# Three seams of an eight-expert block: order of row numbers, one late weight load, the counting product and the last weight halves

## The chip, the cores and the metric

The kernel runs on one core of a Trainium2 chip. The metric is device time in microseconds (us) of one execution; lower is better. Where a time is compared, it is the median over several executions of one kernel, or the time of the one execution that was profiled, and the text says which.

## What is computed

Three stages follow one another. The first is an attention over 4 batches x 8 heads x 576 positions x 64 (a coarse attention over means of 4 positions, plus a local one in a narrow band). Its result, read as 2304 tokens of 512, goes through a mixture of eight experts of which each token takes at most one, and then through a dense two-layer network with a gate. Cut to what matters here:

```python
def _moe_ref(x, w_skip, w_gate, w1, w2):              # 2304 tokens, 512 wide, 8 experts, 1024 hidden
    do_compute = x @ w_skip > 0
    xc = x[do_compute]
    logits = xc @ w_gate
    e_idx = argmax(logits);  gate_w = softmax(logits)[e_idx]
    for e in range(8):
        mask = e_idx == e
        h = maximum(xc[mask] @ w1[e], 0.0)
        y[mask] = gate_w[mask, None] * (h @ w2[e])
    out[do_compute] = xc + y

def _moe2_ref(x, w_in, w_out):                        # 512 -> 2048 -> 512
    h = x @ w_in
    return (h / (1 + exp(-1.702 * h))) @ w_out
```

## The kernel before

**Stages.** Phase A (0 to about 165 us) computes the attention in 16 units (four per batch), writes each unit's tokens to a table `xd` in device memory (`xn` tiles, `L644`), and after the last unit of a batch decides for each token its expert and its place in that expert's list. Phase B (about 165 to 345 us) does the experts. An overflow loop behind it handles tokens beyond an expert's 192 places; its count of passes comes out zero here. Phase C (to the end, 727 us) is the dense network.

**Numbers.** Weights are f32 in memory and are used as two f16 parts: `wh`, the high part (scaled by a power of two, `w_s`), and `wl`, what is left. For each expert there are four half matrices of 1 MB: first layer halves 00 and 01, second layer halves 10 and 11. Each is loaded by SP (`raw`, `L935`), run through a sum of squares on ACT (`jk`, `L951`, function `bound`), from which a small product on PE (`psw`, function `scale`) and six short DVE instructions (`w_e`, `w_s`, `w_i`, and `iv`; function `scale2`, step `scb`) make the scale; then `wh` (`hi`, `L975` on ACT, `L977` on DVE) and `wl` (`lo`, `L983`, always DVE). `scale(i)` makes the scale of expert i's second layer together with that of expert i+1's first layer. The tokens have one scale for all, `sx_s`, made from their largest value `xb` (`xb0` to `xb4`, ending with `xmax`, `L789`).

**An expert's steps.** POOL gathers an expert's 192 token rows (`g0` with 128 rows by the row numbers `idt`, `g1` with 64 rows by `idu`, `L1017`). PE transposes them (`px`, `L1030`, `L1033`), ACT makes the high part `xh` (`L1039`), DVE the low part `xl` (`L1045`). The first layer is three products (`wh xh`, `wh xl`, `wl xh`) into `ph` (`L1063`); ACT makes `hh`, DVE `hl`; the second layer (`py`, `L1086` for the 128 rows and `L1101` for the 64) is scaled by `giv` (gate times scales, `L1110`) into `yr` on ACT, added to the gathered row on POOL (`yadd`) and scattered back to `xd`. For the last expert DVE does `yadd` itself from `py` (`L1142`).

**Row numbers.** `ids` (four DVE instructions, `L766` to `L769`) turns the sums `sa` over all batches into `idt` and `idu`. In phase B, DVE's first `wl` is held behind the instruction that `ex.first` names; before, that is the last of `ids` (`L769`). Its first `wh` (step `hi00` of expert 0) is not held.

**What sets the order.** In phase A a planner walks all steps with priorities and estimated durations and writes the order of every engine; a load is a step that may name others that it waits for (the list with `("xd", ...)` at `L1692`). In phase B each step has a due time in the table `STAGE_B` (in experts, e plus the entry), with exceptions in `head` (expert 0), `mine` (expert 1) and `tail` (expert 7); the steps sorted by these times are the order for PE, ACT, DVE and POOL. SP's own order is chosen when the program is built, by an estimate of when what a transfer waits for is done. At most four groups of table writes of phase A are in flight at a time. `passes` (one product `pc` on PE, four DVE instructions `L1148` to `L1156`) counts the overflow passes from the tokens per expert, `acc`, which are final at the end of phase A; `count` loads the result into a register. It stands at time -1.0, which on DVE is behind `giv` of expert 0 and ahead of `xl` of expert 2.

**Beside the experts,** the weights of phase C are prepared within phases A and B (`win.load`, `win.high`, `win.join`, `win.square`: the `w` and `jw` instructions of `L231` to `L256`).

Of the kernel before, what the change touches and what calls it, by code (L numbers as in the profile page):

```python
# [18 lines left out]
P = 128  # L19
# [358 lines left out]
def phase_a(ctx, tc, c, qk, v, vwin, ex, win, fill, tidy):  # L378
# [382 lines left out]
    def ids(b):  # L761

        z = cp.tile([P, 2, E], F32, name="idz")
        d, d2 = cp.tile([P, 2, E], I32, name="idt"), cp.tile([P, E], I32, name="idu")
        a = c["sa"]
        V.tensor_scalar(z, a[:, :, 1, :], 0.0, float(NT + TB), op0=ALU.is_equal, op1=ALU.mult)  # L766
        V.scalar_tensor_tensor(z, a[:, :, 1, :], float(TB), z, op0=ALU.mult, op1=ALU.add)
        V.scalar_tensor_tensor(d, z, -float(TB), a[:, :, 0, :], op0=ALU.add, op1=ALU.add)
        c["idi"] = V.tensor_scalar(d2, d[:, 1, :], 2.0, c["hf2"], op0=ALU.mult, op1=ALU.add).ins  # L769
        c["id"] = d[:, 0, :], d2  # L770
# [16 lines left out]
    def xb4(u):  # L787
        c["sx"], c["ix"] = pow2_scale(nc, cp, hd["ps"][:, P:P + 1], "sx", True, t=XT)
        V.tensor_scalar(c["xmax"], c["ix"], 2.0 ** XT, None, op0=ALU.mult)  # L789
# [110 lines left out]
    for i, rd in ((-1, (0, 1)), (0, (2, 3, 4, 5))):  # L900
        add(es, i, [("eb", j) for j in rd] + ([("xb4", NU - 1)] if i == 0 else []), [("es", "small", 2)])
        add(ev, i, ["es"], [("ev",)])
# [16 lines left out]
class Experts:  # L919
# [50 lines left out]

    def hi(self, e, wi, hf, on_act):
# [4 lines left out]
        else:  # L976
            self.nc.vector.tensor_scalar(t, r, s, None, op0=ALU.mult)  # L977
        self.h[e, wi, hf] = t

    def lo(self, e, wi, hf):  # L980
# [3 lines left out]
        if self.first is not None:  # L984
            self.tc.add_manual_dep(i.ins, self.first.name,
                                   mybir.DependencyInfo(mybir.DependencyClass.NoSync, mybir.DependencyReason.DATA),
                                   reason="row numbers first")
            self.first = None
# [3 lines left out]
def phase_b(ctx, tc, c, ex, win, wout):  # L992
# [15 lines left out]
    ex.first = c["idi"]  # L1008
# [195 lines left out]
    done += [(0, "scale"), (0, "scb")]  # L1204
    tail = dict(l2b0=-1.23735, l2b1=-1.23734, giv=-1.64, yadd0=-1.22, scatter0=-1.21, ymx=-0.59)
# [9 lines left out]
    for i, t in zip(range(WA, DF // P), (4.5, 4.51, 4.52, 4.53, 5.1, 5.11, 5.12, 5.13)):  # L1215
# [6 lines left out]
    sched.append((-1.0, -2, 0, lambda e: passes()))  # L1222
# [394 lines left out]
def kern(ctx: ExitStack, tc, qk, v, vwin, w_gate, w1, w2, w_in, w_out, out):  # L1617
# [66 lines left out]
    with ab:  # L1684
# [4 lines left out]
        with ea as s:  # L1689
            fill = [(6.4, init, "SP", 0.45, 0.1, (), 0), (-7.6, init1, "SP", 1.3, 0.4, [("xd", 0)], 1)]  # L1690
            fill += [(5.5 + 4 * e + 2 * wi + hf, lambda e=e, wi=wi, hf=hf: [ex.load(e, wi, hf)], "SP", 0.4, 2.75,
                      [("xd", LOADS_A["e"][4 * e + 2 * wi + hf])] + [("wd", j) for j in range(WA // 2) if e == 0], (e, wi, hf))  # L1692
# [62 lines left out]
```

## Time and profile before

| | |
|---|---|
| median of 3 runs | 728.62 us (725.91 to 729.83) |
| the profiled execution | 728.87 us |
| its span, first to last instruction | 727.2 us |
| mean granted PE clock over the span | 0.960 of 2.4 GHz |
| PE busy | 654.9 us, 90% of the span |
| DVE busy | 494.4 us, 68% |
| ACT busy | 425.6 us, 59% |
| POOL busy | 221.5 us, 30% |

A share of busy time is a mean over three stages with different limits. Phase C, more than half of the span, is nearly all PE. The change lies in the stretch from about 118 to 340 us, so the views to read are those of that stretch: the timeline of each engine, which gives an instruction's start, its length, and in brackets the idle time ahead of it and what ended that; the busy time in short windows with the granted clock; and the chain, which starts at the last instruction and follows back what each step waited for.

### The profile page before, as it was taken

What the parts mean: (1) busy time and instruction counts of PE and PEld (TensorE: products, weight loads), DVE (VectorE), ACT (ScalarE), POOL (GpSimd) and SP (SyncE); (2) the same over time, 40 slices, a digit from 0 to 9 for tenths busy, and PEclk for the clock granted to TensorE, in tenths of its full rate; (3) what the DMA queues carried; (4) which work ended last, traced back from release to release, by engine and by line L of the source; (5) the groups of instructions that cost most, each with busy time, mean ns of one, the idle gap of its engine ahead of it and who ended that gap; (6) DMA issues with size and microseconds to landing.
All of it is one profiled execution on the core that took longest, in us unless ns stands there. A gap on an engine that the chain in (4) does not pass through costs nothing.

```text
span 727.2 us, 16364 instructions
## 1 busy us (share of the span) xinstructions
PE 654.9 (90%) x6639; PEld 460.9 (63%) x6639; DVE 494.4 (68%) x1027; ACT 425.6 (59%) x891; POOL 221.5 (30%) x216
## 2 busy tenths in 40 slices
PE   4788988773889999975999999999999999999997
PEld 3576878663767777753666665444974795695443
DVE  6589898865669999977898999975544365063000
ACT  4478787783785888683779794242544364163111
POOL 6686754205546787781000002411000000000000
PEclk9899999975999999997999999999999999999999
DMA  8799976853747777644240411000011000100111
GB/s 302 235 300 294 280 207 224 274 168 109 234 171 274 247 284 283 216 157 129 76 145 16 174 59 43 16 30 29 16 26 47 16 2 15 29 2 1 30 30 30
DMA packets 37889, 94.90 MB, mean 131 GB/s; under 512 B 8861, under 2 KB 22817, under 8 KB 31668
## 3 DMA queue, kind: packets, MB, share of 16 engines
q1 hardware_dynamic: 34996, 88.34, 37.0%
q0 software_dynamic: 2816, 5.50, 2.5%
q8 instruction: 53, 0.87, 0.5%
q14 instruction: 24, 0.20, 0.1%
HBM read 81.91 MB, written 12.92 MB: 130 GB/s over the span
## 4 chain that ended last, share of the span: by engine, by line
PE 55%; DVE 18%; issue 11%; ACT 6%; DMA 6%; POOL 4%; SPq 0%; POOLq 0%; ACTq 0%; DVEq 0%
PE po L1534 17%; PE ph L1437 13%; PE px L1474 7%; DVE wl L983 3%; PE py L1474 3%; PE ph L1063 3%; DMA xd<-xn 3%; DVE v L1406 2%; PE po L576 2%; POOL ids L1172 2%; PE pz L1474 2%; PE px L628 1%; POOL g L1139 1%; DVE wh L977 1%; PE px L1355 1%
## 5 line engine op out<-in xcount | busy, mean ns | idle before, releaser
L1534 PEld LDWEIGHTS <-gh 128*128 128x128 f16 x576 | 56.2, 98 | 66.4 <-issue 1.3
L983 DVE SCALAR_TENSOR_TENSOR wl<-raw,w_s,wh 128x2048 f16<-128x2048 f32 x32 | 76.5, 2422 | 7.8 <-ACT wh L975 6.9
L1437 PE MATMUL ph<-xx,wih 128*128 128x384 f16 x384 | 72.6, 326 | 0.8 <-ACT xx L1369 0.8
L1542 ACT ACTIVATE o<-po,os 128x128 f32<-128x128 f32 x72 | 20.6, 369 | 83.3 <-issue 55.4
L1534 PE MATMUL po<-woh,gh 128*128 128x512 f16 x288 | 65.9, 379 | 1.0 <-ACT o L1542 1.0
L1534 PE MATMUL po<-wol,gh 128*128 128x512 f16 x288 | 65.6, 379 | 0.0
L1534 PE MATMUL po<-woh,gl 128*128 128x512 f16 x288 | 65.4, 379 | 0.0
L951 ACT ACTIVATE jk<-raw 128x2048 f16<-128x2048 f32 x32 | 61.1, 1911 | 6.4 <-issue 4.9
L1403 POOL TENSOR_TENSOR v<-wih,wil 128x512 f32<-128x512 f16 x16 | 18.4, 1151 | 141.4 <-ACT gh L1429 108.0
L1437 PEld LDWEIGHTS <-wih 128*128 128x128 f16 x384 | 37.7, 100 | 23.9 <-issue 1.0
L1534 PEld LDWEIGHTS <-gl 128*128 128x128 f16 x288 | 28.2, 98 | 33.5
L1063 PEld LDWEIGHTS <-wh 128*128 128x128 f16 x512 | 44.6, 101 | 6.4 <-issue 5.4
L975 ACT ACTIVATE wh<-raw,w_s 128x2048 f16<-128x2048 f32 x18 | 35.2, 1995 | 20.0 <-DVE w_s L80 17.3
L1485 DVE TENSOR_TENSOR q<-pz,q 128x192 f32<-128x192 f32 x24 | 8.6, 358 | 54.7 <-ACT q L1483 49.1
L1437 PE MATMUL ph<-xx,wil 128*128 128x384 f16 x192 | 39.2, 326 | 0.0
L1139 POOL TENSOR_TENSOR g<-g,yr 128x512 f32<-128x512 f32 (+1 forms) x14 | 30.3, 2162 | 26.8 <-ACT yr L1123 26.6
L1441 ACT ACTIVATE sg<-ph,ih 128x384 f32<-128x384 f32 x48 | 27.7, 577 | 17.0 <-PE ph L1437 16.2
L1063 PE MATMUL ph<-xh,wl 128*128 128x192 f16 x256 | 33.2, 253 | 2.8 <-DVE wl L983 1.8
L1430 DVE SCALAR_TENSOR_TENSOR gl<-sg,gs,gh 128x384 f16<-128x384 f32 x48 | 31.0, 646 | 6.3 <-ACT gh L1429 6.0
L1063 PE MATMUL ph<-xl,wh 128*128 128x192 f16 x256 | 33.5, 254 | 1.9 <-DVE xl L1045 1.1
L1474 PEld LDWEIGHTS <-sh 128*128 128x128 f16 x384 | 34.0, 98 | 1.2 <-issue 0.5
L1063 PE MATMUL ph<-xh,wh 128*128 128x192 f16 x256 | 33.5, 255 | 1.2 <-ACT xh L1039 1.0
(262 smaller groups left out, 1649.3 us busy)
## 6 DMA issues: line engine op xcount, KB each, us to landing
raw<-in_moe_w SPq DMA_DIRECT2D x32, 1024.0 KB
vw<-in_vwin SPq DMA_DIRECT2D x16, 576.0 KB
qk<-in_qk SPq DMA_DIRECT2D x16, 576.0 KB
w<-in_moe_w_in SPq DMA_DIRECT2D x8, 1024.0 KB
w<-in_moe_w_out SPq DMA_DIRECT2D x8, 1024.0 KB
vn<-in_v SPq DMA_DIRECT2D x16, 288.0 KB
xd<-xn SPq DMA_DIRECT2D x16, 288.0 KB
x<-xd SPq DMA_DIRECT2D x18, 256.0 KB
```

The lines of the kernel that those rows point to most:

```text
L951: self.nc.scalar.activation(j, r, AF.Square, accum_out=self.mx[i][:, hf, wi:wi + 1])
L975: self.nc.scalar.activation(t, r, AF.Copy, scale=s)
L983: i = self.nc.vector.scalar_tensor_tensor(t, r, s, self.h[e, wi, hf], op0=ALU.mult, op1=ALU.subtract)
L1063: T.matmul(ph[:, fi, :], wa[:, k_, o:o + P], xa[:, k_, :], start=(n == 0), stop=(n == 3 * NK - 1))
L1139: G.tensor_tensor(g, g, yr[e][:, cols(ti)].rearrange("p (h w) -> p h w", w=DM // 2), ALU.add)
L1403: G.tensor_tensor(v, h, l, ALU.add)
L1430: V.scalar_tensor_tensor(split[2], split[0], split[3], split[1], op0=ALU.mult, op1=ALU.subtract)
L1437: T.matmul(ph, win.chunk(wa, f)[:, k_, :], xx[:, k_, :], start=(n == 0), stop=(n == 3 * NK - 1))
L1441: A.activation(sg, ph, AF.Gelu_apprx_sigmoid, scale=ih[:, f // 4:f // 4 + 1])
L1474: T.matmul(o, w[:, k_], xx[:, at + k_], start=(first and i + k_ == 0), stop=(i + k_ == 3), skip_group_check=not first)
L1534: T.matmul(po, ga[:, f, i * P:(i + 1) * P], wa[:, f, :], start=(n == 0), stop=(n == 3 * (DF // P) - 1))
L1542: A.activation(o[:, sl], po[:, sl], AF.Copy, scale=os_[:, j:j + 1])
```

## The change

It has five parts.

1. Phase B's first `wh` and first `wl` on DVE are both held behind `xmax`, the last instruction of the token scale, instead of the first `wl` alone behind `idu`.
2. The scale of expert 0's second layer and expert 1's first layer leaves the plan of phase A and becomes a step of phase B like those of the other experts.
3. The load of expert 1's second first-layer half (1, 0, 1) waits for the last batch's gates (`("gs", B - 1)`, the `gt` tiles).
4. `passes` moves from -1.0 to -5.97, among the first steps of phase B.
5. For expert 7, `scb`, `hi11` and `lo11` come earlier, so that both second-layer halves are made in one go, and the eight `win.high` steps come later.

```diff
 def ids(b):
-        c["idi"] = V.tensor_scalar(d2, d[:, 1, :], 2.0, c["hf2"], op0=ALU.mult, op1=ALU.add).ins
+        V.tensor_scalar(d2, d[:, 1, :], 2.0, c["hf2"], op0=ALU.mult, op1=ALU.add)
 def xb4(u):
-        V.tensor_scalar(c["xmax"], c["ix"], 2.0 ** XT, None, op0=ALU.mult)
+        c["last"] = V.tensor_scalar(c["xmax"], c["ix"], 2.0 ** XT, None, op0=ALU.mult).ins
...
-    for i, rd in ((-1, (0, 1)), (0, (2, 3, 4, 5))):
-        add(es, i, [("eb", j) for j in rd] + ([("xb4", NU - 1)] if i == 0 else []), [("es", "small", 2)])
-        add(ev, i, ["es"], [("ev",)])
+    add(es, -1, [("eb", 0), ("eb", 1)], [("es", "small", 2)])
+    add(ev, -1, ["es"], [("ev",)])
...
+    def in_turn(self, i):
+        if self.first is not None:
+            self.tc.add_manual_dep(i.ins, self.first.name,
+                                   mybir.DependencyInfo(mybir.DependencyClass.NoSync, mybir.DependencyReason.DATA),
+                                   reason="row numbers and scale first")
+            self.first = None
 def hi(self, e, wi, hf, on_act):
-            self.nc.vector.tensor_scalar(t, r, s, None, op0=ALU.mult)
+            self.in_turn(self.nc.vector.tensor_scalar(t, r, s, None, op0=ALU.mult))
...
-    ex.first = c["idi"]
+    ex.first = c["last"]
...
-    done += [(0, "scale"), (0, "scb")]
-    tail = dict(l2b0=-1.23735, l2b1=-1.23734, giv=-1.64, yadd0=-1.22, scatter0=-1.21, ymx=-0.59)
+    tail = dict(scb=-2.2805, hi11=-2.11, lo11=-1.891, l2b0=-1.23735, l2b1=-1.23734, giv=-1.64, yadd0=-1.22, scatter0=-1.21, ymx=-0.59)
...
-    for i, t in zip(range(WA, DF // P), (4.5, 4.51, 4.52, 4.53, 5.1, 5.11, 5.12, 5.13)):
+    for i, t in zip(range(WA, DF // P), (5.272, 5.273, 5.274, 5.275, 5.276, 5.277, 5.39, 5.41)):
         word(t, win.high, i)
...
-    sched.append((-1.0, -2, 0, lambda e: passes()))
+    sched.append((-5.97, -2, 0, lambda e: passes()))
...
-                      [("xd", ...)] + [("wd", j) for j in range(WA // 2) if e == 0], (e, wi, hf))
+                      [("xd", ...)] + [("wd", j) for j in range(WA // 2) if e == 0] + [("gs", B - 1)] * (hf == e == 1), (e, wi, hf))
```

What moves on the engines is shown at three places.

**SP, end of phase A.** `xd<-gt_97` are the last batch's gates, `raw` the experts' weights, `TENSOR_LOAD tot` the register load of the overflow count. Lines with - stand in the kernel before, lines with + in the changed one.

```order
 L755 DMA xd<-gt_97 96x6x8 x2
-L935 DMA raw<-in_moe_w 128x2048 x6
-L1160 TENSOR_LOAD tot
-L1160 ISA x2
-L935 DMA raw<-in_moe_w 128x2048 x16
+L934 DMA raw<-in_moe_w 128x2048 x3
+L1162 TENSOR_LOAD tot
+L1162 ISA x2
+L934 DMA raw<-in_moe_w 128x2048 x22
```

Twenty-two loads stood behind the gates and 25 stand there now. The three that are new there stood, before, some ten transfers further up, between the load of `w_2271` and a write `xd<-xn`, as `L935 DMA raw<-in_moe_w 128x2048 x3`: (1, 0, 1) and the two first-layer halves of expert 2, which wait for nothing. The register load has three weight loads ahead of it behind the gates, where it had six.

**DVE, where phase A ends and phase B begins.** First the kernel before, from the token maximum `xb`; then, before still, the place of the counting instructions, behind `giv` of expert 0; then the changed kernel, from `t_2947` on.

```order
L774 TENSOR_REDUCE xb<-xm 128x1
L977 TENSOR_SCALAR wh<-raw,w_s 128x2048
L723 TENSOR_TENSOR sa<-sa,sel 128x32
L766 TENSOR_SCALAR idz<-sa 128x16
L767 SCALAR_TENSOR_TENSOR idz<-sa,idz 128x16
L768 SCALAR_TENSOR_TENSOR idt<-idz,sa 128x16
L769 TENSOR_SCALAR idu<-idt,hf_102 128x8
L782 TENSOR_REDUCE xb_2930<-psm 1x1
L729 SCALAR_TENSOR_TENSOR t_2932<-mn,r_2212 96x6
L983 SCALAR_TENSOR_TENSOR wl<-raw,w_s,wh 128x2048
```

```order
L1110 TENSOR_TENSOR giv<-g_3004,iv 128x1
L1110 TENSOR_TENSOR giv<-g_3005,iv 128x1
L1148 COPY cnt<-pc 128x8
L1151 TENSOR_TENSOR gt<-cnt,thr 128x136
L1154 TENSOR_REDUCE sums<-gt 128x1
L1156 CAST tot<-sums 128x1
L1045 SCALAR_TENSOR_TENSOR xl<-px,sx_s,xh 128x768
L983 SCALAR_TENSOR_TENSOR wl<-raw,w_s,wh 128x2048 x2
```

```order
L729 SCALAR_TENSOR_TENSOR t_2947<-mn,r_2877 96x6
L983 TENSOR_SCALAR wh<-raw,w_s 128x2048
L730 TENSOR_TENSOR t_2947<-t_2947,cf 96x6
L989 SCALAR_TENSOR_TENSOR wl<-raw,w_s,wh 128x2048
L1150 COPY cnt<-pc 128x8
L731 TENSOR_SCALAR slt<-t_2947 96x6
L729 SCALAR_TENSOR_TENSOR t_2951<-mn,r_2667 96x6
L1153 TENSOR_TENSOR gt<-cnt,thr 128x136
L730 TENSOR_TENSOR t_2951<-t_2951,cf 96x6
L1156 TENSOR_REDUCE sums<-gt 128x1
L731 TENSOR_SCALAR slt<-t_2951 96x6
L1158 CAST tot<-sums 128x1
```

The row numbers (`sa` to `idu`) and the token scale (to `xmax`) now stand ahead of the first `wh`, and the four counting instructions stand behind the first `wl`, ahead of expert 0's `xl`, instead of ahead of expert 2's. On PE the product `pc` moves likewise, from behind the first layer of expert 1 to just ahead of expert 0's `px`.

**ACT, the last expert.** `w_4629` to `w_4880` are weights of phase C, `wh` here the second-layer halves of expert 7, `yr` the results of expert 6. First before, then changed.

```order
L1069 ACTIVATE hh<-ph 128x384 x2
L252 ACTIVATE w_4629<-w_4629 128x512 x2
L252 ACTIVATE w_4631<-w_4631 128x512 x2
L975 ACTIVATE wh<-raw,w_s 128x2048
L1123 ACTIVATE yr<-py,giv 128x512
L1123 ACTIVATE yr<-py,giv 128x256
L1069 ACTIVATE hh<-ph 128x384
L252 ACTIVATE w_4878<-w_4878 128x512 x2
L252 ACTIVATE w_4880<-w_4880 128x512
L1069 ACTIVATE hh<-ph 128x384
L252 ACTIVATE w_4880<-w_4880 128x512
L975 ACTIVATE wh<-raw,w_s 128x2048
```

```order
L1071 ACTIVATE hh<-ph 128x384 x2
L981 ACTIVATE wh<-raw,w_s 128x2048 x2
L1125 ACTIVATE yr<-py,giv 128x512
L1125 ACTIVATE yr<-py,giv 128x256
L1071 ACTIVATE hh<-ph 128x384 x2
L252 ACTIVATE w_4629<-w_4629 128x512 x2
L252 ACTIVATE w_4631<-w_4631 128x512 x2
L252 ACTIVATE w_4878<-w_4878 128x512 x2
L252 ACTIVATE w_4880<-w_4880 128x512 x2
```

Both `wh` stand together ahead of `yr`, and the eight instructions for phase C behind the last `hh`. On DVE the scale steps of the last expert come ahead of two `hl`, and the two `wl` follow one another.

## Rows read from the trace of the kernel before

**Rows 1.** Page, section 4: share of each engine in the chain that ended last

```profile
PE 55%; DVE 18%; issue 11%; ACT 6%; DMA 6%; POOL 4%; SPq 0%; POOLq 0%; ACTq 0%; DVEq 0%
```

**Rows 2.** The chain, 110 to 185 us: start, us, engine, what

```profile
121.93 12.41 DMA xd<-xn
...
161.26 4.72 DMA xd<-gt
```

**Rows 3.** Timeline, SP: start, us of issuing, transfer, count

```profile
118.93 2.38 SPq L935 DMA_DIRECT2D raw<-in_moe_w  x3
...
156.50 0.45 SPq L935 DMA_DIRECT2D raw<-in_moe_w  x1
...
160.91 0.88 SPq L755 DMA_DIRECT2D xd<-gt  x2
```

**Rows 4.** Windows: stretch, us, busy PE, PEld, DVE, ACT, POOL, clock, DMA, GB/s

```profile
120.00:123.00 3.00, 3.00 (x96) 2.71 (x94) 2.86 (x10) 2.99 (x7) 0.00 (x0) 1.00 1.03 420
147.00:150.00 3.00, 2.44 (x11) 2.47 (x12) 2.23 (x15) 2.78 (x8) 0.00 (x0) 0.50 0.03 5
188.00:192.00 4.00, 2.07 (x12) 1.11 (x10) 3.71 (x2) 2.21 (x3) 3.14 (x3) 0.89 0.22 35
229.95:247.63 17.68, 17.68 (x187) 13.93 (x185) 16.83 (x21) 14.93 (x18) 13.37 (x8) 1.00 0.81 298
```

**Rows 5.** Timeline of ACT, DVE and POOL, 140 to 190 us

```profile
140.69 0.80 ACT L638 COPY xn<-px 96x768 f32<-96x768 f32 x1 [1.06 <-DMA xd<-xn]
164.11 1.91 ACT L951 ACTIVATE jk<-raw 128x2048 f16<-128x2048 f32 x1 [1.13 <-DMA raw<-in_moe_w]
166.09 2.00 ACT L975 ACTIVATE wh<-raw,w_s 128x2048 f16<-128x2048 f32 x1
176.62 0.90 ACT L1039 ACTIVATE xh<-px,sx_s 128x768 f16<-128x768 f32 x1 [6.63 <-PE px L1033]
...
166.46 1.29 DVE L977 TENSOR_SCALAR wh<-raw,w_s 128x2048 f16<-128x2048 f32 x1 [3.28 <-DMA xd<-gt]
168.30 0.17 DVE L768 SCALAR_TENSOR_TENSOR idt<-idz,sa 128x16 int32<-128x16 f32 x1
168.92 2.33 DVE L983 SCALAR_TENSOR_TENSOR wl<-raw,w_s,wh 128x2048 f16<-128x2048 f32 x1
...
169.55 2.75 POOL L1017 DMA_INDIRECT g<-xd,idt  x1 [10.59 <-DVE t L729]
172.60 0.95 POOL L1017 DMA_INDIRECT g<-xd,idu  x1 [0.30 <-DVE sx_i L81]
189.50 1.94 POOL L1172 DMA_INDIRECT ids<-tok,slt  x1 [0.31 <-issue]
```

**Rows 6.** Timeline of ACT, DVE and PE around the counting product, 204 to 219 us

```profile
204.43 3.90 ACT L975 ACTIVATE wh<-raw,w_s 128x2048 f16<-128x2048 f32 x2 [2.21 <-DVE w_s L80]
...
210.27 0.17 DVE L1148 COPY cnt<-pc 128x8 f32<-128x8 f32 x1 [5.41 <-PE pc L1147]
...
212.26 0.49 PE L1063 MATMUL ph<-xl,wh 128*128 128x192 f16 x4 [0.86 <-DVE xl L1045]
214.53 0.51 PE L1063 MATMUL ph<-xh,wl 128*128 128x192 f16 x4 [1.77 <-DVE wl L983]
...
215.98 0.85 PE L1063 MATMUL ph<-xh,wl 128*128 128x192 f16 x4
```

**Rows 7.** Timeline of ACT, DVE and PE in the last expert, 314 to 335 us

```profile
321.78 2.00 ACT L975 ACTIVATE wh<-raw,w_s 128x2048 f16<-128x2048 f32 x1
...
314.77 0.15 DVE L75 TENSOR_SCALAR w_e<-psw 128x2 int32<-128x2 int32 x1
323.82 3.08 DVE L983 SCALAR_TENSOR_TENSOR wl<-raw,w_s,wh 128x2048 f16<-128x2048 f32 x1 [1.68 <-ACT wh L975]
334.90 0.48 DVE L1142 SCALAR_TENSOR_TENSOR g<-py,giv,g 128x256 f32<-128x256 f32 x1 [0.52 <-DVE w L233]
...
326.95 0.59 PE L1086 MATMUL py<-wl,hh 128*128 128x512 f16 x2 [2.52 <-DVE wl L983]
```

More of the change, by code (lines that the diff above doesn't have):

```diff
@@ L983, in lo @@
         i = self.nc.vector.scalar_tensor_tensor(t, r, s, self.h[e, wi, hf], op0=ALU.mult, op1=ALU.subtract)
[L984 to L988, printed above, removed]
+        self.in_turn(i)
         self.l[e, wi, hf] = t
@@ L1691, in kern @@
             fill += [(5.5 + 4 * e + 2 * wi + hf, lambda e=e, wi=wi, hf=hf: [ex.load(e, wi, hf)], "SP", 0.4, 2.75,
-                      [("xd", LOADS_A["e"][4 * e + 2 * wi + hf])] + [("wd", j) for j in range(WA // 2) if e == 0], (e, wi, hf))
+                      [("xd", LOADS_A["e"][4 * e + 2 * wi + hf])] + [("wd", j) for j in range(WA // 2) if e == 0] + [("gs", B - 1)] * (hf == e == 1), (e, wi, hf))
                      for e in range(2) for wi in range(2 - e) for hf in range(2)]
```

## The prediction

> **What bounds the kernel now.** I read three views in this order. The chain's shares by engine [rows 1]: PE holds 55% of the way to the last instruction, DVE 18%, transfers 6%, and "issue" 11%. PE's part is mostly the dense network, which the change does not touch, so the question is what PE waits for earlier. The busy windows answer it: in the middle of the experts PE is busy 17.68 of 17.68 us per expert, at clock 1.00 (2.4 GHz), while DVE has 16.83 [rows 4]. There PE cannot be helped; a gain must come from places where PE waits or has a low clock. The timelines show four: the seam from attention to routing, where a table write sits 12.41 us behind loads [rows 2] and PE runs at clock 0.50 (1.2 GHz) afterwards [rows 4]; the first gather, for which everything in the experts waits [rows 5]; the counting product, which leaves DVE idle for 5.41 us [rows 6]; and the last expert, where PE waits 2.52 us for a `wl` [rows 7]. The sum goes against the profiled execution, 728.87 us; the median is 728.62, so the two can be taken as one.
>
> **Part by part.**
>
> *The late load.* Before, a load of phase C's weights and three expert loads, 4 MB, stand ahead of the write issued at 121.93 [rows 2, 3]; at the 420 GB/s of the next window [rows 4] 4 MB take 10.0 us, which is most of its 12.41. ACT then waits 1.06 us for that write before its next `xn` [rows 5]. The order shows that 3 of the 4 MB go, some 7.5 us, so this write ends well before ACT asks. Taken: -1.1 us, the wait itself. Bounds: 0, if the next wait swallows it; and -3.6, if PE also keeps a higher clock there. The window at 147 has clock 0.50 with 2.44 of 3 us busy [rows 4]; at the full clock about half of that, with waits kept, returns in two such stretches, 2.5 us. I take the end nearer the wait, because PE falls to 0.50 after waiting for a chain of DVE and ACT steps that stays.
>
> The same 3 MB now start behind the gates, whose write is issued at 160.91 and takes 0.88 [rows 3], thus at about 161.8, beside the first gathers. At 420 GB/s they take 7.5 us; the load of 156.50 ended when ACT's `jk` could start at 164.11 [rows 3, 5], so the three end at about 167 to 172 (estimate). ACT has a `jk` that reads the first of them (1.91 us) and a `wh` (2.00) [rows 5] ahead of `xh`: 167.6 + 0.2 + 4 gives 171.8, while `xh` can start at 176.62 less the gain of the next step, 174.3. Cost 0, with 2.5 us of cover.
>
> *Row numbers first.* Before, DVE's first `wh` started at 166.46, when the gates had landed (161.26 + 4.72 = 165.98), and `idt` came behind it at 168.30 to 168.47 [rows 2, 5]. The gather needs both the gates and `idt`. After, `idt` stands ahead of `wh` and is ready before the gates, so the release moves from 168.5 to about 166. The gather itself began at 169.55 and took 2.75 us while DVE ran `wl` (168.92 to 171.25); the second, with DVE at other work, took 0.95, and a third POOL transfer at 189.50, beside a `wl`, took 1.94 [rows 5]. So a gather started beside a long DVE instruction ends with it. After, the first starts at 166.5, together with `wh` (to 167.75), and ends about 168.7; the second meets `wl`, which now ends at 170.3, and ends at 171.2, against 173.55. Gain 2.35. Bounds: -4.85, if neither is held (171.2 less 2.5), and +0.1, if the short DVE instructions that now stand first (twenty of about 0.17 us) delay `wh`. Behind the gathers everything to the first product moves: `px`, `xh`, `ph`. I take -2.35, since the two rows with a `wl` beside the transfer agree.
>
> By the Trainium skill's page "SBUF — State Buffer", section "SBUF: two separate sides", a VectorE instruction with two SBUF inputs and a GpSimd one lock each other out of a shared port for the whole instruction, and a software-issued transfer cannot write its descriptors meanwhile. The rows of 2.75 against 0.95 agree. By the strict form the gathers would wait for both `wh` and `wl`; this is the third rival below.
>
> *The scale of expert 0's second layer.* Two products and seven DVE instructions (about 1.4 us) move behind expert 0's first `hl`. They are the same work; `wh` of the second layer needs them only after the first layer. Cost 0, bounded by +0.9 if PE must wait once more as it did for `xl` [rows 6].
>
> *The counting product.* DVE's copy stands idle 5.41 us for `pc`, which PE reaches only behind expert 1's first layer; `xl` of expert 2 and two `wl` stand behind it. PE then waits 0.86 and 1.77 us and, after that, falls to a lower clock: groups of four matmuls take 0.85 us against 0.49 [rows 6]. Four such groups cost 4 x 0.36 = 1.4, their slower neighbours some 0.3. Moved to the head, the copy waits for nothing: `acc` is final long before, and its four instructions (some 0.9 us) lie between `wl` and `xl` at 171 to 172, while DVE waits for `xh` anyway. At expert 2, DVE gains more (ACT's second `wh` ends at 208.33, so the second `wl` could move from 214.6 to 208.8, 5.8 us), but PE, which is full before 210 and after 219, returns only its own loss: 0.86 + 1.77 + 1.7 and the wait within the groups, 4.3 to 4.6. Taken: -4.5. Bounds: -2.6 (the two waits, clock as before) and -6.35 (5.41 and the four instructions, if DVE were the bound).
>
> On SP the register load of the count now has only three loads ahead of it and waits for DVE until about 172; the next load behind it waited before for the gathers until past 173. Cost 0.
>
> *The last expert.* Before, ACT's second `wh` ran at 321.78 to 323.78, `wl` started at 323.82, took 3.08, and PE waited 2.52 for it; the end of the chain is DVE's last `yadd`, at 334.90 [rows 7]. After, the scale steps start some 0.9 us before 314.77 (two `hl` no longer stand ahead), ACT makes both `wh` at about 315 to 319, DVE both `wl` at 317 to 321.6, then `hl`, `ym`, `hl` to 323.5. The three joins and two `yadd` that follow stood from 326.9 to 335.4; they now start at 323.8, three us earlier, and PE is ready for them since its wait is gone. `yr` of expert 6 comes 1.0 us later; POOL's add and scatter behind it end well before DVE's last `yadd`. Gain 3.3. Bounds: -2.3, if POOL's add slows DVE's pair of `wl` to 3.08 each; -5.0, if the 0.5 us waits between the joins go too.
>
> **Sum:** -1.1 - 2.35 - 4.5 - 3.3 = -11.25; 728.87 - 11.25 = 717.6 us. The dense network behind it keeps its length, give or take 1.5 us, since there PE's order changes in small places only.
>
> **The rivals.**
>
> - *More comes back at the head* (0.15). Between 188 and 192 PE is busy only 2.07 of 4 us, with waits that no other instruction ends [rows 4]. If this goes away with the new timing, or the clock holds at the seam, 3.6 us more: 714.0. Against it: nothing in the change removes instructions there.
> - *The seams are eaten* (0.13). The three loads and the gathers run together, and `jk` on the late load stands first on ACT; if that gives back exactly the first two terms, 3.45 us, the time is 721.1. For it: one write waited 12.41 us behind 4 MB. Against it: the gathers go by another queue. By the Trainium skill's page "DMA: Bandwidth & Descriptors", section "Queues, rings and completion order", a DMA engine takes turns between queues packet by packet, so a gather would not wait for the loads; no row here shows the two side by side.
> - *DVE holds both gathers* (0.10). If the first cannot finish before `wl` has, at 170.3, both end 1.05 us earlier instead of 2.35: 718.9. The rows with 2.75 and 1.94 speak for it, that `wh` reads one tensor only speaks against it.
> - *Only the last expert stays* (0.06). The change does at the head not what it says: PE, arriving earlier, waits as long elsewhere, for instance for the loads of expert 1 and 2 that now come later. Then -3.3 alone: 725.6.
> - *Slower* (0.04). ACT works in order, so a late `raw` at the head of its queue stops `wh` and `xh` of expert 0. The other three terms are worth 8.9 us; it breaks even when `xh` starts at 185.5, hence when the load lands at 181.4, 19.6 us after its issue. The longest wait in the queue is 12.41 [rows 2]. At twice that, `xh` starts at 190.7, 14.1 later than before: 734.1. For it speaks only that three loads are issued at once.
>
> **How the numbers follow.** The forecast has 0.52: 717.6 us. To hold 8 in 10 the range takes the forecast with its bounds, the held gathers, the eaten seams and half of the better head: 713 to 722. A measurement of this kernel can tell about 0.5%, 3.6 us, from no change. The forecast, the first three rivals and no other lie beyond that on the fast side, 0.90; the fourth is within it, 0.06; the fifth beyond it, 0.04.
>
> **What would show it.** Right: the first gather starts near 166.5 less a microsecond and the second ends near 170; DVE's counting copy shows no wait and PE no gap at expert 2, and the clock stays 1.00 there; in the last expert no PE wait of 2.5 us, the last `yadd` some 11 us earlier than 334.90. Wrong: ACT's `jk` ahead of the first `xh` shows an idle time for its load longer than 2.5 us; gathers of 4 us or more; PE gaps of the same size at expert 1 or 2 under another releaser; or a dense network that is longer by more than 2 us.

## The result, and the profile after

The changed kernel took 718.95 us (median of 6 runs, 716.53 to 726.74), the kernel before 727.83 beside it; the ratio is 0.9891 with a 95% interval of 0.9851 to 0.9931. On a second occasion it was 0.9867 (0.9818 to 0.9916). The forecast was 717.6 us, range 713 to 722. Its profiled execution took 717.3 us with a span of 715.6, against 728.87 and 727.2.

One caution belongs ahead of every reading below. The kernel before, run against itself as if it were another kernel, came out at 0.9946 (0.9900 to 0.9991), and its runs spread from 714.9 to 732.7 us. So a ratio here can be off by half a percent, 3.9 us, by nothing at all, and one profile can be off by nearly as much in one stretch. I therefore took a second profile of both kernels and read each stretch from all of them. The stretches, from the start of one instruction to the start of the next:

| stretch, us | before | before, second | changed | changed, second |
|---|---|---|---|---|
| start to the load of `w_2271` | 118.45 | 119.25 | 116.74 | 118.42 |
| to the write of the last gates | 42.46 | 43.62 | 41.48 | 41.71 |
| to the first `ph` | 16.66 | 15.24 | 16.23 | 16.31 |
| to `px` of expert 3 | 32.49 | 29.92 | 31.26 | 28.93 |
| to `px` of expert 7 | 74.68 | 73.27 | 69.38 | 70.48 |
| to the last `yadd` | 50.16 | 49.01 | 47.04 | 46.80 |
| to the end | 392.30 | 393.09 | 393.47 | 392.95 |
| span | 727.2 | 723.4 | 715.6 | 715.6 |

Between the means the change is worth -9.7 us: -1.3 in the first row, where both kernels have the same instructions in the same order and all 14 profiles lie anywhere from 115.7 to 121.9 (chance, then), -1.5 at the seam, +0.3 at the head, -1.1 in the fourth row, -4.1 at the counting product, -2.7 in the last expert, +0.5 in the dense network.

The page of the changed kernel, section 1 (busy time, share of the span, instructions):

```profile
PE 650.3 (91%) x6639; PEld 458.8 (64%) x6639; DVE 494.6 (69%) x1027; ACT 425.5 (59%) x891; POOL 221.3 (31%) x216
```

The work is the same as before, in number and nearly in busy time; what has changed is waiting. The timeline of the changed kernel at the seam and the head, to be held against [rows 5]: start, us, engine, line, what, and in brackets the idle time ahead and what ended it.

```profile
139.40 0.80 ACT L638 COPY xn<-px 96x768 f32<-96x768 f32 x1
...
166.25 1.91 ACT L950 ACTIVATE jk<-raw 128x2048 f16<-128x2048 f32 x1 [2.37 <-DMA raw<-in_moe_w]
168.16 1.99 ACT L981 ACTIVATE wh<-raw,w_s 128x2048 f16<-128x2048 f32 x1
173.50 0.90 ACT L1041 ACTIVATE xh<-px,sx_s 128x768 f16<-128x768 f32 x1 [3.35 <-issue]
...
161.91 0.17 DVE L768 SCALAR_TENSOR_TENSOR idt<-idz,sa 128x16 int32<-128x16 f32 x1
164.59 1.29 DVE L983 TENSOR_SCALAR wh<-raw,w_s 128x2048 f16<-128x2048 f32 x1 [0.15 <-DMA raw<-in_moe_w]
165.91 2.35 DVE L989 SCALAR_TENSOR_TENSOR wl<-raw,w_s,wh 128x2048 f16<-128x2048 f32 x1
168.18 0.16 DVE L1150 COPY cnt<-pc 128x8 f32<-128x8 f32 x1
...
164.92 1.98 POOL L1019 DMA_INDIRECT g<-xd,idt  x1 [8.65 <-DMA raw<-in_moe_w]
167.21 1.88 POOL L1019 DMA_INDIRECT g<-xd,idu  x1 [0.30 <-issue]
...
171.92 1.09 PE L1032 MATMUL px<-ident,g 128*128 128x128 f32 x4 [8.31 <-DMA g<-xd,idt]
```

`xn` has no wait any more (1.06 before). `idt` is early, the gather starts 4.6 us sooner (1.9 of it counted from the write of the gates), the count's copy waits for nothing. ACT's `jk` waits 2.37 us for the late load, but `xh` does not come from that: ACT is idle again for 3.35 us ahead of it. The surprise is the last row. The first gather's issue is over at 166.90 and `px` starts only at 171.92, 5.0 us later; in [rows 5] the issue was over at 172.30, and the trace before has `px` 2.5 us behind that:

```profile
174.79 1.09 PE L1030 MATMUL px<-ident,g 128*128 128x128 f32 x4 [4.72 <-issue]
```

The timeline of the changed kernel in the last expert and ahead of the dense network, against [rows 7]:

```profile
305.71 3.90 ACT L981 ACTIVATE wh<-raw,w_s 128x2048 f16<-128x2048 f32 x2 [1.78 <-DVE w_s L80]
...
307.75 4.61 DVE L989 SCALAR_TENSOR_TENSOR wl<-raw,w_s,wh 128x2048 f16<-128x2048 f32 x2 [0.68 <-ACT wh L981]
322.13 0.48 DVE L1144 SCALAR_TENSOR_TENSOR g<-py,giv,g 128x256 f32<-128x256 f32 x1 [0.80 <-DVE w L233]
...
327.35 0.37 PE L67 MATMUL psm<-ident,x2m 128*1 128x128 f32 x1 [9.00 <-DVE x2m L1321]
332.90 1.44 PE L1438 MATMUL ph<-xx,wih 128*128 128x384 f16 x4 [0.78 <-ACT xx L1370]
334.14 1.48 PE L1438 MATMUL ph<-xx,wil 128*128 128x384 f16 x4
```

The `wl` follow one another and PE's wait of 2.52 us is gone; PE is through by 318.4, but then waits 9.00 us, and its first groups in the dense network are 1.24 to 1.28 us apart.

### The profile page after: what moved, and what is told of

Its sections match the earlier page's. It is cut to its first block, busy times and chain, and to the rows that moved or that the text cites. A ratio compares the mean times of both kernels' runs of the same rounds, so it can differ in the third digit from the quotient of the medians.

```text
span 715.6 us, 16372 instructions
## 1 busy us (share of the span) xinstructions
PE 650.3 (91%) x6639; PEld 458.8 (64%) x6639; DVE 494.6 (69%) x1027; ACT 425.5 (59%) x891; POOL 221.3 (31%) x216
## 4 chain that ended last, share of the span: by engine, by line
PE 46%; DVE 14%; issue 9%; ACT 4%; POOL 4%; DMA 2%; ACTq 0%; POOLq 0%; SPq 0%
PE po L1535 17%; PE ph L1438 13%; PE px L1475 7%; DVE wl L989 4%; PE py L1475 3%; DVE v L1407 2%; POOL ids L1174 2%; PE pz L1475 2%; ACT wh L981 2%; DVE wh L983 1%; DVE hl L1075 1%; PE px L1356 1%; DVE sl L1414 1%; DMA raw<-in_moe_w 1%; POOL g L1141 1%
## 5 line engine op out<-in xcount | busy, mean ns | idle before, releaser
L1141 POOL TENSOR_TENSOR g<-g,yr 128x512 f32<-128x512 f32 (+1 forms) x14 | 28.4, 2028 | 22.6 <-ACT yr L1125 22.4
L1174 POOL DMA_INDIRECT ids<-tok,slt x24 | 32.6, 1357 | 7.3 <-issue 7.3
```

The lines of the kernel that those rows point to most:

```text
L1141: G.tensor_tensor(g, g, yr[e][:, cols(ti)].rearrange("p (h w) -> p h w", w=DM // 2), ALU.add)
L1174: d = G.indirect_dma_start(c["ids"], IOA(ap=c["slt"][:TB, j:j + 1], axis=0), c["tok"][:TB, j:j + 1], None, bounds_check=RMAX - 1, oob_is_e ...
```

## The experiments

Each kernel is the changed one with one edit, unless it says otherwise. Ratios are to the kernel before, on the same chip; those of four in one group may be compared with each other. The groups: the counting product put back, the last expert put back, no wait for the gates, `wh` and `wl` as before; the counting product moved alone, the joins, expert 2's loads later, `wh` behind the gathers; both kernels once more, the products in the pause, the edits together.

### The counting product put back, and moved alone

```diff
-    sched.append((-5.97, -2, 0, lambda e: passes()))
+    sched.append((-1.0, -2, 0, lambda e: passes()))
```

> The changed kernel with the counting product alone put back to its old place, behind the first layer of expert 1. Theory (the counting term, worth 4.5 us on PE): DVE's copy of the count is idle again some 5 us, PE waits for xl and wl of expert 2 some 2.6 us in two gaps and has groups of 0.85 us behind them, so the profiled time is 4 to 5 us above the 717.3 of the changed kernel, 721.3 to 722.3. Rival (PE would be held there by something else anyway, the first layer halves of expert 2 that are now loaded later): less than 1.5 us above.

Measured: ratio 0.9938 (0.9907 to 0.9969), profiled span 719.5. Timeline of DVE and PE, and one window (columns as in [rows 4]):

```profile
205.07 0.17 DVE L1150 COPY cnt<-pc 128x8 f32<-128x8 f32 x1 [3.79 <-PE pc L1149]
...
205.74 0.66 PE L1032 MATMUL px<-ident,g 128*128 128x128 f32 x4 [0.73 <-ACT yr L1125]
209.36 0.50 PE L1065 MATMUL ph<-xh,wl 128*128 128x192 f16 x4 [1.80 <-DVE wl L989]
...
206.00:209.00 3.00, 1.55 (x16) 0.98 (x14) 3.00 (x3) 3.00 (x5) 2.41 (x3) 1.00 0.15 61
```

DVE's idle time and PE's gap for `wl` are back; the gap for `xl` is not, nor has the second profile of before it. In the changed kernel the same window has PE full:

```profile
206.00:209.00 3.00, 3.00 (x38) 2.77 (x37) 3.00 (x5) 3.00 (x4) 2.72 (x2) 1.00 0.83 330
```

From `px` of expert 3 to that of expert 7 it takes 73.18 us, as in the two profiles of before (74.68, 73.27), against 69.38 to 70.75 in the eleven others. The clock in this run stays at 1.00, so of the 4.5 us the slow groups are the part that comes and goes. Two kernels of its group that keep the product at the head have ratios of 0.9895 and 0.9898, some 3 us less.

The reverse, the kernel before with the same line changed to -5.97:

> The kernel before with the counting product alone moved to the head. Theory: 4 to 5 us less than 728.87, 723.9 to 724.9, with no PE gap at expert 2 and the clock at 1.00 there. Rival (the counting product only uncovers the waits that the seam and the loads make): less than 2 us.

Measured: ratio 0.9971 (0.9934 to 1.0008), profiled span 718.9. In the profile PE has no wait in that stretch, which takes 70.75 us, 2.5 to 3.9 us less than before; the timing shows 2.1 us, with an interval that reaches zero. The profiled time, 720.58 us, is 8.3 us below 728.87 where 4 to 5 were expected; the rest lies in other stretches, most of it from the first `ph` to the first `py` (16.0 us, where the first profile of before has 19.9). The step is confirmed in its place; its size is 2.5 to 4 us by the profiles, and timing does not narrow it further.

### The last expert put back

```diff
-    tail = dict(scb=-2.2805, hi11=-2.11, lo11=-1.891, l2b0=-1.23735, l2b1=-1.23734, giv=-1.64, yadd0=-1.22, scatter0=-1.21, ymx=-0.59)
+    tail = dict(l2b0=-1.23735, l2b1=-1.23734, giv=-1.64, yadd0=-1.22, scatter0=-1.21, ymx=-0.59)
...
-    for i, t in zip(range(WA, DF // P), (5.272, 5.273, 5.274, 5.275, 5.276, 5.277, 5.39, 5.41)):
+    for i, t in zip(range(WA, DF // P), (4.5, 4.51, 4.52, 4.53, 5.1, 5.11, 5.12, 5.13)):
```

> The changed kernel with the last expert's order alone put back. Theory: PE's gap of about 2.5 us before py and the slow groups behind it come back, DVE's last yadd comes 2.9 us later against the px of expert 5 than in the changed kernel, and PE's pause before the dense network shrinks from 9.0 to about 6.4 us. Profiled time 2.3 to 3.3 us above 717.3 if the dense network keeps its length; 1.5 to 2.5 above if the longer pause is what made the dense network 1.15 us longer in the changed kernel (rival on where that 1.15 went).

Measured: ratio 0.9925 (0.9887 to 0.9963), profiled span 720.6. Its timeline of PE, with the product that ends PE's pause (`psm`):

```profile
321.19 0.66 PE L1088 MATMUL py<-wl,hh 128*128 128x512 f16 x2 [1.90 <-DVE wl L989]
321.64 1.06 PE L1088 MATMUL py<-wh,hl 128*128 128x512 f16 x2
...
333.82 0.37 PE L67 MATMUL psm<-ident,x2m 128*1 128x128 f32 x1 [5.88 <-DVE x2m L1321]
...
339.45 0.81 PE L1438 MATMUL ph<-xx,wih 128*128 128x384 f16 x4 [0.78 <-ACT xx L1370]
340.10 0.81 PE L1438 MATMUL ph<-xx,wil 128*128 128x384 f16 x4
```

Gap and slow groups are back; `px` of expert 7 to the last `yadd` is 49.07 us, against 46.80 to 47.25 in the kernels with the new order. So the order is worth 2.2 us there (3.1 against the first profile of before, in which `wl` took 3.08). And the dense network starts fast here, groups 0.65 us apart; from its first `px` to the end it takes 384.97 us (384.57 in the kernel with the counting product alone), against 386.1 to 386.8 in those with the new order. The second profile of before has the old order and also 386.1, but it has the longer pause too:

```profile
335.47 0.37 PE L67 MATMUL psm<-ident,x2m 128*1 128x128 f32 x1 [7.54 <-DVE x2m L1320]
...
340.94 1.44 PE L1437 MATMUL ph<-xx,wih 128*128 128x384 f16 x4 [0.78 <-ACT xx L1369]
342.18 1.48 PE L1437 MATMUL ph<-xx,wil 128*128 128x384 f16 x4
```

So in the twelve profiles without added products the slow start goes with the length of PE's pause, not with the order as such: three have a pause of 5.88 to 6.41 us, groups 0.65 us apart from the start and 384.6 to 385.3 us to the end; nine have 7.14 to 9.01 us, first groups 1.23 to 1.24 us apart and 386.1 to 387.4 us. The profiled time, 722.33 us, is more than was expected; 2.55 us of it lie ahead of any edit (the load of `w_2271` starts at 119.29, against 116.74).

### Products laid into PE's pause

```diff
+    def warm(n, x, w):
+        pw = psh.tile([P, 512], F32, tag="psh", name="pw")
+        for _ in range(n):
+            T.matmul(pw[:, 0:w], c["ones"], x, start=True, stop=True)
+    sched.append((E - 1 - 1.1, -2, 1, lambda e: warm(28, ex.h[E - 1, 1, 1][:, 0, :], 512)))
```

> The changed kernel with 28 products more on PE behind the last py, whose result nobody reads, about 6 us of work laid into PE's pause ahead of the dense network. Theory (of the last expert's gain some 1.6 us are given back in the dense network, because PE now pauses 9 us instead of 6.4 and comes back at clock 0.50): the window behind the first px of the dense network shows 1.00, groups of ph 0.65 us apart from the start, and the dense network is 1.5 to 2.5 us shorter, 384.0 to 385.1 us from its first px to the end; the whole gains as much over the changed kernel. Rival (the dense network is longer for its weights, prepared later): it stays at 386 to 387 us.

Measured: ratio 0.9945 (0.9907 to 0.9983), that is slower than the changed kernel beside it (0.9867). Its timeline of PE, and the window behind the first `px` of the dense network:

```profile
320.95 6.22 PE L1163 MATMUL pw<-wh,ones 128*128 128x512 f16 x28
332.23 0.37 PE L67 MATMUL psm<-ident,x2m 128*1 128x128 f32 x1 [5.06 <-DVE x2m L1327]
337.32 1.44 PE L1444 MATMUL ph<-xx,wih 128*128 128x384 f16 x4 [0.78 <-ACT xx L1376]
...
333.54:337.54 4.00, 3.23 (x14) 2.49 (x14) 3.74 (x14) 2.31 (x4) 0.00 (x0) 0.50 0.52 148
```

A miss. The products kept the clock at 1.00 while they ran, but the pause behind them is still 5.06 us, and PE comes back at 0.50 all the same. And from the last `yadd` to the dense network's first `px` it now takes 9.14 us instead of 6.9: `x2m` on DVE, behind the overflow loop through which every engine has to pass, comes later. So the run does not decide whether the pause is the cause; it shows only that PE comes back slow from this shorter one too, and that PE's place ahead of that loop isn't free.

### The joins behind the last `yadd`

```diff
-    for i, t in zip(range(WA, DF // P), (5.38, 5.4, 5.8, 6.45, 6.46)):
+    for i, t in zip(range(WA, DF // P), (6.42, 6.43, 6.44, 6.45, 6.46)):
         word(t, win.join, i)
```

> The changed kernel with the joins of phase C's weights put behind the last expert's yadd and its maximum on DVE. Theory (in the changed kernel the end of the experts is no longer PE but DVE, which has three joins of 1.9 to 2.5 us ahead of and between the two yadd): the last yadd follows PE's end at 318.5, 3 to 3.5 us earlier, and the time falls by 2 to 3.5 us, 713.8 to 715.3. Rival (the joins come due in the dense network, whose weights are then late): within 1 us of 717.3 or above.

Measured: ratio 0.9922 (0.9888 to 0.9957), profiled span 718.5. Timeline of DVE and PE:

```profile
321.76 0.48 DVE L1144 SCALAR_TENSOR_TENSOR g<-py,giv,g 128x256 f32<-128x256 f32 x1 [2.00 <-PEq L1243]
328.56 0.16 DVE L1321 TENSOR_REDUCE x2m<-ym 128x1 f32<-128x10 f32 x1 [3.87 <-issue]
...
331.15 2.98 PE L1356 MATMUL px<-ident,x 128*128 128x128 f32 x12 [0.66 <-DMA x<-xd]
```

The first half of the theory holds: the last `yadd` comes 43.59 us behind `px` of expert 7 instead of 46.8 to 47.3, begun 0.1 us behind PE's last product. The second doesn't: behind it `x2m` waits 3.87 us (2.06 in the changed kernel), the first `px` of the dense network follows at 9.39 us instead of 6.9, and that network takes 387.35 us. What was gained is given back, so the joins are not what sets the end. What the loop between the two stages waits for in this kernel, the trace does not name.

### The head: which of loads and DVE delays the gather

Four edits, one at a time: the late load without its wait for the gates; the two first-layer loads of expert 2 held back until the gathers of expert 0 are in; DVE's first `wh` held back until then; DVE's first `wh` and `wl` as in the kernel before.

```diff
-                      [("xd", ...)] + [("wd", j) for j in range(WA // 2) if e == 0] + [("gs", B - 1)] * (hf == e == 1), (e, wi, hf))
+                      [("xd", ...)] + [("wd", j) for j in range(WA // 2) if e == 0], (e, wi, hf))
```

```diff
-                ex.last.setdefault((1, 1, 0), []).append(d)
+                for z in ((1, 1, 0), (2, 0, 0), (2, 0, 1)):
+                    ex.last.setdefault(z, []).append(d)
```

```diff
-    head = dict(hi00=-6.0, hi01=-5.99, lo00=-5.98)
+    head = dict(gather=-6.1, hi00=-6.0, hi01=-5.99, lo00=-5.98)
...
+                ex.pool = d
...
+            if self.pool is not None:
+                self.tc.add_manual_dep(i.ins, self.pool.ins.name,
+                                       mybir.DependencyInfo(mybir.DependencyClass.Sync, mybir.DependencyReason.DATA),
+                                       reason="after the gathers")
```

```diff
-        V.tensor_scalar(d2, d[:, 1, :], 2.0, c["hf2"], op0=ALU.mult, op1=ALU.add)
+        c["idi"] = V.tensor_scalar(d2, d[:, 1, :], 2.0, c["hf2"], op0=ALU.mult, op1=ALU.add).ins
...
-            self.in_turn(self.nc.vector.tensor_scalar(t, r, s, None, op0=ALU.mult))
+            self.nc.vector.tensor_scalar(t, r, s, None, op0=ALU.mult)
...
-    ex.first = c["last"]
+    ex.first = c["idi"]
```

> The changed kernel without the wait of the late load for the gates: the three loads go back up ahead of the table write. Theory of the seam (load queue): ACT waits about 1 us for that write again, the gates are issued 1.3 to 2.7 us later, but no load runs beside the first gathers, so px starts about 2.5 us behind the end of the gather's issue instead of 5.0; net 0 to +1.5 us, 717.3 to 718.8. Rival (the landing of 5.0 us is due to DVE's wh and wl beside it): px still 5 us behind, net +2.7, 720.0.

> The changed kernel with the two first-layer loads of expert 2 also waiting for the gathers of expert 0, so that one load instead of three runs beside these gathers. Theory (loads delay the landing of the gathers): px starts 2.5 to 3.5 us behind the end of the first gather's issue instead of 5.0, some 1.5 to 2.5 us earlier, and the whole gains 1 to 2.5 us, 714.8 to 716.3, unless expert 2's halves come too late. Rival (DVE's wh and wl delay it): px unchanged within 0.5 us.

> The changed kernel with DVE's first wh waiting for the first two gathers, so that no long DVE instruction runs beside them. Theory (loads delay the landing): the gathers are issued in 0.95 us each, but px starts at 170 to 172 all the same, wh and wl come 5 to 6 us later, PE waits for wl, 1 to 3 us above 717.3. Rival (DVE delays the landing by keeping descriptors from being written): px starts near 168.5, 2.5 us behind the gather, and the whole is within 1 us of 717.3 or below.

> The changed kernel with DVE's first wh no longer held and wl behind the row numbers alone, as before. Theory (row numbers): idt comes some 1.5 to 2.5 us later and px with it at most as much, since the gather also waits for its landing beside the loads: 0.5 to 2.5 us above 717.3. Rival (the gather's landing is set by the three loads, not by its start): no change, within 0.5 us.

Measured, beside the kernel before and the changed one (us; gates is the start of the write of the last gates):

| kernel | ratio | gates to gather | its issue | end of issue to `px` | gates to first `ph` |
|---|---|---|---|---|---|
| before; second profile | 1; 0.9946 | 8.64; 7.27 | 2.75; 2.75 | 2.49; 2.42 | 16.66; 15.24 |
| changed; second profile | 0.9891; 0.9867 | 6.70; 6.31 | 1.98; 1.52 | 5.02; 5.94 | 16.23; 16.31 |
| no wait for the gates | 0.9895 | 6.56 | 1.52 | 3.15 | 14.17 |
| expert 2's loads later | 0.9881 | 6.70 | 1.52 | 2.94 | 14.46 |
| `wh` behind the gathers | 0.9965 | 4.98 | 1.16 | 6.11 | 14.78 |
| `wh`, `wl` as before | 0.9898 | 8.83 | 2.75 | 3.39 | 17.51 |

The intervals of the four are 0.984 to 0.995, 0.982 to 0.995, 0.994 to 1.000 and 0.985 to 0.995. The rows behind the deciding column, of POOL and PE: first the run in which no long DVE instruction stands beside the gather, then the one in which one load instead of three runs beside it.

```profile
163.79 1.16 POOL L1023 DMA_INDIRECT g<-xd,idt  x1 [7.63 <-DVE sx_e L79]
...
171.06 1.08 PE L1037 MATMUL px<-ident,g 128*128 128x128 f32 x4 [7.73 <-DMA g<-xd,idt]
177.20 0.80 PE L1070 MATMUL ph<-xl,wh 128*128 128x192 f16 x4 [2.81 <-DVE xl L1052]
```

```profile
170.26 1.52 POOL L1019 DMA_INDIRECT g<-xd,idt  x1 [8.65 <-DMA raw<-in_moe_w]
...
174.72 1.09 PE L1033 MATMUL px<-ident,g 128*128 128x128 f32 x4 [6.64 <-DMA g<-xd,idt]
```

This decides it. With DVE quiet the gather is issued in 1.16 us, yet lands 6.1 us later; with DVE as in the changed kernel but two of the three loads away, it lands in 2.9. DVE stretches the issue (2.75 beside `wl`, 1.5 to 2.0 beside `wh`, 1.16 beside neither), the loads stretch the landing. The two microseconds behind the end of the issue show the loads themselves, in the last column (GB/s): first the changed kernel, then the one with expert 2's loads later.

```profile
166.90:168.90 2.00, 0.00 (x0) 0.00 (x0) 2.00 (x7) 2.00 (x3) 1.70 (x1) 0.50 1.00 420
171.80:173.80 2.00, 0.00 (x0) 0.00 (x0) 2.00 (x7) 2.00 (x3) 1.71 (x1) 0.50 0.51 135
```

By the packet times in the traces, the gather's first data packet comes 0.7 us behind the end of its issue where the loads are through by then or nearly so (seven profiles, the one with `wh` and `wl` as before among them), and 2.0 to 3.1 us behind it where 1.0 to 1.8 MB of the loads still pass before `px` (the other seven). The row numbers brought forward are worth 2.5 us at the end of the issue (10.0 to 11.4 us behind the gates before, 7.8 to 8.7 after), and the three loads, put beside the gather by part 3 of the change, take as much back. The fourth run is the check: row numbers late, loads still beside, and 17.51 is the longest of all.

In the whole time the first, the second and the fourth are not told from the changed one: the intervals overlap almost wholly. The third is slower; its `wl` comes later, and PE waits 2.81 us for the `xl` behind it. The totals that were expected decide nothing here: the run with expert 2's loads later took 720.28 us in its profile, where 714.8 to 716.3 was expected, with 5.2 us of it ahead of any edit, and the run with `wh` behind the gathers 717.64, where 718.3 to 720.3 was. Without the wait for the gates the earlier seam comes back too, since `xn` waits 1.39 us for its write again.

### Both kernels once more, and the edits together

> The kernel before once more, for a second profile of it on the chip of these four runs. The profile of before from which the prediction was made has stretches that the other runs with the same instructions there do not show: 19.9 us from the first ph to the first py (16.0 to 18.7 in the other runs). If that was a chance of the one execution, this run shows 16 to 18.7 there and a ratio of 1 to itself; if it belongs to the kernel before, 19 or more.

> The changed kernel once more, on the same chip as the other three. Ratio to before 0.985 to 0.993; gates' write to first ph 16 to 17.3 us; PE's pause before the dense network 9 us and, after it, four groups of ph in the dense network 1.28 us apart instead of 0.65.

Measured: 0.9946 and 0.9867, spans 723.4 and 715.6; their stretches are in the first table. From the first `ph` to the first `py` the second profiles have 16.5 and 16.4 us where the first had 19.9 and 18.7. In both first profiles PE's products come singly for two to three us there, with idle time that no other engine ended [rows 4]; in both second ones that is absent. It belongs to the execution, not to either kernel.

The last run holds expert 2's loads back, and lays 48 short products on PE between the counting product and the first `px`, besides the 28 of above:

```diff
+    sched.append((-5.965, -2, 1, lambda e: warm(48, c["ones"], 128)))
```

> The changed kernel with three things more: expert 2's two first-layer loads wait for the gathers of expert 0, 48 short products on PE lie between the counting product and the first px, 28 between the last py and the dense network. Theory: gates' write to first ph 14 to 14.8 us instead of 16 to 17.3, groups of ph of expert 0 0.33 us apart from the start (2 us less), dense network 384 to 385 us; together 4 to 6.5 us below the changed kernel, ratio to before 0.977 to 0.984. Rival (what is gained at the head is waited for at expert 1 and 2, whose weights come no sooner): 2 us below it.

Measured: ratio 0.9892 (0.9838 to 0.9945), span 715.3. Timeline of PE:

```profile
162.29 4.91 PE L1164 MATMUL pw<-ones 128*128 128x128 f16 x48
169.09 0.63 PE L1033 MATMUL px<-ident,g 128*128 128x128 f32 x4 [1.90 <-ACT jk L950]
171.09 0.47 PE L1036 MATMUL px<-ident,g 64*128 64x64 f32 x4 [1.38 <-DMA g<-xd,idu]
172.62 0.80 PE L1066 MATMUL ph<-xh,wh 128*128 128x192 f16 x4 [1.05 <-ACT xh L1042]
173.67 0.80 PE L1066 MATMUL ph<-xl,wh 128*128 128x192 f16 x4 [0.26 <-DVE xl L1048]
```

The first `ph` comes 14.70 us behind the gates, as expected, and the first `px` group runs fast (0.63 us against 1.08), but behind the short waits of 1.38 and 1.05 us that follow the groups are slow again, 0.64 us apart. The forecast of 4 to 6.5 us below the changed kernel was a miss. The last `yadd` is at 319.19, and from there to the end it takes 396.1 us instead of 393: the second set of products costs what it cost above. No version was shown to beat the changed kernel.

## Why the prediction was right, and where it wasn't

**The late load** (term -1.1): right. From one `xn` to the next on ACT it takes 3.60 and 3.71 us where it took 4.23 and 4.94, and the wait of 1.06 to 1.27 us is absent in every kernel that has the load behind the gates and back (1.39) in the one that hasn't. To the gates' write it is -1.5 us between the means. That the clock would fall there all the same was right as well: it is 0.50 from 146 to 149 us in the first profile of the changed kernel and from 150 to 152 in the second.

**Row numbers first** (term -2.35): wrong, the head gains nothing, 16.3 us from the gates to the first `ph` against 15.2 and 16.7. The working of the issue was right in its result: a gather started beside a long DVE instruction is drawn out, though it ends about 1 us behind that instruction and not with it, in [rows 5] too. What failed is the step before it, "Cost 0, with 2.5 us of cover": I priced the three loads only for ACT, by `jk` and `xh`, where the cover did hold, and let the gather land 2.5 us behind its issue as before. It lands 5.0 to 5.9 us behind it. This is the second rival, for the half that lies at the head; the half at the seam stayed. I had set against that rival that the gathers go by another queue. By the Trainium skill's page "DMA: Bandwidth & Descriptors", section "Queues, rings and completion order", the engines take turns between queues; the trace agrees in that packets of the gather pass before the last load packet, and shows that its landing doubles all the same, with its first packet 2.0 and 2.6 us behind the issue in the two profiles of the changed kernel instead of 0.7.

**Which lock.** By the Trainium skill's page "SBUF — State Buffer", section "SBUF: two separate sides", a VectorE instruction with two SBUF inputs and a GpSimd one that reads SBUF exclude each other for an instruction's length; that no descriptors can be written meanwhile it states of VectorE's two-port modes, and the prediction put the two together. The rows go with the lock for the issue: 2.75 and 1.87 us beside `wl`, which reads two tensors, 1.16 and 0.95 beside short ones. `wh`, which reads one, holds a gather as well: in the changed kernel it ends at 165.88, and the first gather, begun beside it at 164.92, ends at 166.90, 1.0 us behind `wh` and in the middle of `wl`. In all thirteen profiles where the first gather starts beside a `wh` or a `wl` it ends 1.03 to 1.04 us behind that instruction. So the third rival, that the first gather cannot finish before `wl` has, did not come true: it ended 1.4 us before `wl`, about as the forecast had it (168.7, 0.95 behind `wh`).

**The scale of expert 0's second layer and the register load on SP** (0): right. PE waits for neither. SP stands 6.1 us at the register load until the count is there, but the load behind it then waits 1.9 us more for the second gather, so the count is not what holds it.

**The counting product** (term -4.5): right in kind, and a little large. Copy without wait, no gap on PE; -4.1 between the means of the stretch, -2.5 to -3.9 by undoing it or moving it alone, near the lower bound of 2.6 where the clock holds. That PE, not DVE's 5.8 us, sets the gain held.

**The last expert** (term -3.3): right in kind, too large. At the last `yadd` it is -2.2 to -3.1. The term read the end from a profile in which `wl` took 3.08 us; in the second profile of before it takes 2.47, and PE waits 1.91 instead of 2.52. A part, about 1.2 us between the means of the profiles with the old and the new order (385.2 and 386.5 us), goes again in the dense network, which with the new order begins with PE at clock 0.50 after a pause of 8.6 to 9.0 us; the working had no term for it beyond its 1.5 us of slack. That the pause causes it is not shown: the twelve profiles go with it, and the run with products in the pause, slow behind 5.06 us, does not.

**The sum.** Forecast -11.25. The first pair of profiles gives -11.6, which looks like a hit and is partly luck: -1.7 of it fell ahead of the first edit, and -1.2 where a stall came shorter. With two profiles each, and the first row of the table left out, it is -8.4 us; the timed ratios give 0.9867 to 0.9891 of 728, -8 to -9.7 us. The three terms that held come to 8.3 us by the table, 8.9 in the sum, and the head to nothing.

## What to carry to other kernels

When a transfer is moved out of the way of one consumer, list every transfer that will run beside it at its new place, those of other queues too, and price their landing, not just who reads the moved one. A small product put in the middle of full engines costs what waits behind it in order, and belongs where its inputs are ready and its readers idle. And before a profile's stretch is explained, take a second profile of the same kernel: here one stretch differed by 3 us between two executions.

## What the runs showed of the hardware

A gather of 128 rows landed 2.4 to 3.15 us behind its issue with no load left beside it, 3.4 where the loads were nearly through, and 5.0 to 6.3 us beside three loads of 1 MB. Begun beside a DVE instruction of 128x2048, whether with one input or two, its issue ended 1.03 to 1.04 us behind that instruction. With identical instructions, phase A's gates were written anywhere from 157.5 to 163.6 us in the profiles of kernels with the changed order. In the last run PE's groups of four products of 192 columns stood 0.64 us apart, the slow pace, behind waits of 1.90, 1.38 and 1.05 us, although 48 products had run ahead of these.
